# The first layer of the second MLP in float16 parts, its weights converted during the first MLP and kept in DRAM

## The chip, the cores and the metric

One core of one Trainium2 chip. The metric is the device time of one execution in microseconds, the median of the runs shown. Five engines work side by side, each with its own queue: PE (matrix products), DVE (vector), ACT (scalar functions), POOL, and SP, which issues all the DMAs of this kernel.

## The reference

```python
def _moe_ref(x, w_in, w_out):
    h = x @ w_in
    g = np.maximum(0.01 * h, h)
    return (g @ w_out).astype(np.float32)

def _moe2_ref(x, w_in, w_out):
    h = x @ w_in
    g = h * (1.0 / (1.0 + np.exp(-h)))
    return (g @ w_out).astype(np.float32)
...
    attn_out = _attn_ref(**attn_kwargs)
    x = np.ascontiguousarray(attn_out.transpose(0, 2, 1, 3)).reshape(B * S, H * D)
    x = _moe_ref(x=x, **moe_kwargs)
    return _moe2_ref(x=x, **moe2_kwargs)
```

The attention has 4 x 8 heads of 576 positions and 64 columns with a mask by blocks of 64. Both MLPs have 2304 tokens, a model width of 512 and an inner width of 2048. The weights come as 64-bit floats, everything else as 32-bit floats.

## The kernel before

The tokens are cut into six blocks of 384, numbered 0 to 5. The work has four stages on PE. First comes the attention of block 0 and the first MLP of block 0 in full precision. Then blocks one to five of the first MLP run while PE also works on the attention of the next block; each block has 16 steps (one per 128 inner columns), and a step is 12 products of the first layer (lines 1785 to 1787) and 12 of the second (line 1814). Each float32 operand there is a sum of two float16 parts, high and low, and a product is three matmuls: low by high, high by low, high by high.

Stage three is the first layer of the second MLP. It takes two blocks at a time (b = 0, 1, 2; 768 tokens) and two of the 16 inner tiles at a time (pair i = 0 to 7), and replaces the eight products of a 2 x 2 split by seven, after Strassen and Winograd, at the price of sums of operands and results. `add_first(b, i)` (line 2051) is one such unit: seven products, each of two halves of the contraction by three matmuls, 42 in all, of 128 x 384 (lines 2064 to 2066). Its operands are kept as high and low parts of type float32r. The sums over the results are made by DVE (lines 2089 to 2100), then ACT applies the Silu (line 2116) and takes squares of the result (line 2125), from whose largest a scale for stage four is found. Stage four is the second layer, again with seven products, in float16 parts (line 2243).

The order on each engine is written out ahead by a planner (`Schedule`, line 73). Every operation is a task with its possible engines and their estimated times, its dependencies and a rank; an engine that comes free takes the ready task of the lowest rank. Products of PE that belong to the two MLPs keep the order of the program (`in_turn`). A rank with `GATE` (-1000) is first, with `SHORT` (-500) next; then come plain ranks. A plain rank is the number of the step (block times 16 plus step) plus an offset, or, in stage three, `unit3(b, i)`, 96 plus 1.75 a unit. The attention's tasks have `rank_at`, made of `ATT` and `ATT_SLOPE`.

What the change touches, by name and line:

- `convert` (432) loads 128 x 512 weights of 64 bits (512 KB) into one of three `raw` places and makes 32-bit floats of them: a scaling on ACT (449), a shift on DVE or ACT (454, 456), and a join on DVE (460). It takes turns in two `cy` and two `cc` places.
- `first_pair(p)` (748) converts the two inner tiles of a pair for the first layer, makes four sums on DVE (`s1` to `s4`, 256 columns each) and splits 3.5 x 512 columns into high (402) and low (413) parts of float32r, all of it after the attention has ended. `last_raw(p)` (789) converts those of the second layer during stage three, takes their squares (806) and stores the four pieces in DRAM (`w2_kept`). `last_pair(p)` (924) reads them back and splits them by `scaled_split` (704: high part at 710, on ACT alone; low part at 715, on DVE) into places that earlier units have freed; its rank has `GATE`.
- `find_range` (851) turns a set of sums of squares into a power of two: a maximum over columns (DVE), a spread (ACT or DVE), a DMA transpose, another maximum and four one-column operations (DVE).
- `x_operands(b)` (1989) loads the first MLP's results for two blocks, makes four sums and splits seven operands of 768 columns into the `x3` places, which have one buffer each: for b > 0 an operand is rewritten after its last use in unit (b - 1, 7) and before its use in unit (b, 0).
- `add_second` (1876) is a step's second layer; in a block's last step it also evacuates four banks into y (1921, 1923) in places given by `YRINGS`, and stores them.

```python
                for k in (0, 1):
                    w, x = slice(k * P, (k + 1) * P), slice(k * n, (k + 1) * n)
                    nc.tensor.matmul(o, wlo[:, w], xhi[:, x], start=k == 0, stop=False)
                    nc.tensor.matmul(o, whi[:, w], xlo[:, x], start=False, stop=False)
                    nc.tensor.matmul(o, whi[:, w], xhi[:, x], start=False, stop=k == 1)
```

Of the kernel before, what the change touches and what calls it, by code (L numbers as in the profile page):

```python
# [19 lines left out]
P = 128  # L20
# [10 lines left out]
LATE = 10  # L31
# [18 lines left out]
W2_BEFORE, W2_MID = 2, 5  # L50
W2_AHEAD, X2_AHEAD, X2_FIRST, LAST_AHEAD = 18, 7, 14, 5
LAST_FROM, LAST_TO = 1, 14
# [193 lines left out]
def attn_mlp_mlp(  # L246
# [110 lines left out]

    def next_s():
        return ps_s.tile([P, 512], F32, tag="s", name="s")
# [69 lines left out]
    raws, cys, ccs = Turns(RAWS), Turns(CYS), Turns(CCS)  # L429

    def convert(src, f, sl, rk, load_rank, to=None, slow=0, lag=0, free=()):
# [4 lines left out]
        raw_free, raw_after, raw_users = raws.next()  # L436
# [3 lines left out]
        def load():  # L440
            r = raw_room().bitcast(I64)
# [23 lines left out]
        t_load = dma(raw_free, load_rank, DM * P * 8, load, after=[*raw_after, *raw_later], slow=slow, lag=lag)  # L465
        raws.takers.append(t_load.issue)
# [184 lines left out]
    class Place:  # L651


        def __init__(self, make, deps):
            self.make, self.deps, self.tile, self.halves = make, deps, None, None

        def view(self, a, n):
            if self.tile is None:
                self.tile = self.make(F32R)
            return self.tile[:, a : a + n]  # L660

        def half(self, a, n):
            if self.halves is None:
                self.halves = self.make(F16)
            return self.halves[:, 2 * a : 2 * a + n]

    def second_places():

        if w2_places:
            return  # L670
        for k in range(LATE - 1):
            place = Place(lambda t, k=k: late(k, t), [end_of_attention])
            w2_places.extend([(place, 0), (place, DM)])
        w2_places.append((Place(lambda t: late(LATE, t, n=DM), [end_of_attention]), 0))
        place = Place(lambda t: area("xw", "r" if t == F32R else "rh", t), ())
        place.step = slot_of("xw")[-1]
        w2_places.append((place, 2 * TWO))
        for k in (27, 28, 29, *range(9), *range(11, NF)):
            place = Place(lambda t, k=k: slot(k, "r" if t == F32R else "rh", t), ())
            place.step = k  # L680
            w2_places.extend([(place, 0), (place, DM)])
        assert len(w2_places) == 7 * NF // 2 - 2
        place = Place(lambda t: late(LATE - 1, t), ())
        place.step = None
        w2_places[7 * NF // 2 - 2 :] = [(place, 0), (place, DM)]

    def place_of(p, k, halved=False):

        second_places()
        at, over = 7 * p + k, 0  # L690
        if halved and (at == 2 * LATE - 1 or p % 2 == 0 and k == 6):
            at, over = at - 1 if k < 6 else at - 3, DM
        place, at = w2_places[at]
        deps = place.deps
        if hasattr(place, "step"):
            deps = y_there[NBLK - 2][:2] if place.step is None else slot_free(place.step)
        if halved:
            return deps, (lambda n=DM, a=0: place.half(at, over + a + n)[:, over + a :])
        return deps, (lambda n=DM, a=0: place.view(at + a, n))
# [3 lines left out]
    def high_on(n):  # L703
        return {"ACT": act(n, False, 1)}
# [18 lines left out]
    def seven_parts(p, whole, piece, rk, more=()):  # L723

        deps, get = zip(*(place_of(p, k) for k in range(7)))
        got, tasks = [], []
        for k, (n, value, t) in enumerate(whole):
            hi, lo = get[2 * k], get[2 * k + 1]  # L730
            ts = split(n, value, lambda hi=hi, lo=lo: (hi(), lo()), [*t, *deps[2 * k], *deps[2 * k + 1], *more], rk)
            got.append((hi, lo))
            tasks.append(ts)
        make, value = piece
        t4 = make(tasks)
        last = get[6]
        ts = split(H2, value, lambda: (last(H2), last(H2, H2)), [t4, *deps[6], *more], rk)
        tasks.append(ts)

        def operand(k, half):  # L740
            if k == 3:
                return last(H2), last(H2, H2)
            hi, lo = got[k]
            return hi(H2, half * H2), lo(H2, half * H2)

        return operand, tasks, t4

    w2_places = []
    w2_first, w2_last, w2_done1, w2_done2 = {}, {}, {}, {}

    def first_pair(p):

        rk = unit3(0, p) - W2_AHEAD
# [9 lines left out]
        def s2(e):  # L763
            rest(e, d["t"][:, H2:], d["t"][:, :H2], d0["x"][:, :H2])
# [1691 lines left out]
```

## Time and profile before

| | us |
|---|---|
| median of three runs | 877.36 (876.89 to 879.8) |
| the profiled execution | 878.52 |
| its span, first to last instruction | 876.8 |
| PE busy | 860.7 |
| DVE busy | 751.4 |
| ACT busy | 623.8 |
| matmuls | 6569 |

The page gives busy times over the whole span. The views by stretch, the chain of waits and the timelines show where the span goes. A matmul's own duration in the profile overlaps the next one's, so that the pace of PE is read from the distance of starts.

### The profile page before, as it was taken

Reading aid. Unit: us, or ns where it says so; the run is one execution under the profiler, and the core shown is the slowest. Engines: PE = TensorE matmul, PEld = TensorE weight load, DVE = VectorE, ACT = ScalarE, POOL = GpSimd, SP = SyncE. Lnnn points to the kernel's source line nnn. Section 1 sums busy time; section 2 is a strip of 40 time slices with the busy share of each in tenths; the row PEclk is TensorE's granted clock in tenths of the full one; section 3 lists DMA queues with packets and bytes.
Section 4 is the critical chain, followed back from the end, with each engine's and each line's share of the span. In section 5 each row is a group of like instructions: output and inputs, shape, how many; then the busy total and the mean of one; then the engine's idle time right before and its main releaser. Section 6 shows DMA issues by size and latency. Waiting matters only on the chain.

```text
span 876.8 us, 18274 instructions
## 1 busy us (share of the span) xinstructions
PE 860.7 (98%) x6569; PEld 648.6 (74%) x6569; DVE 751.4 (86%) x1700; ACT 623.8 (71%) x1434; POOL 14.9 (2%) x75
## 2 busy tenths in 40 slices
PE   8899999999999999999999999999999999999997
PEld 4655566666666666666666668999999978888886
DVE  6899989999988998888847399888787999998976
ACT  6899987777766877777636368898897985444433
POOL 0000000000000000000000000000000000000000
PEclk9999999999999999999999999999999999999999
DMA  8689866667776679764534145687858784544431
GB/s 292 212 210 280 238 149 167 135 137 144 174 175 130 141 156 196 165 150 119 109 107 145 71 137 189 231 283 266 290 194 270 271 254 136 177 144 133 159 108 61
DMA packets 179467, 155.77 MB, mean 178 GB/s; under 512 B 108592, under 2 KB 155440, under 8 KB 179376
## 3 DMA queue, kind: packets, MB, share of 16 engines
q1 hardware_dynamic: 179376, 154.61, 63.2%
q8 instruction: 51, 0.84, 0.4%
q14 instruction: 40, 0.33, 0.1%
HBM read 93.85 MB, written 35.65 MB: 148 GB/s over the span
## 4 chain that ended last, share of the span: by engine, by line
PE 79%; DVE 9%; ACT 6%; DMA 3%; issue 2%; DVEq 0%; POOL 0%; ACTq 0%; POOLq 0%; SPq 0%
PE acc L1814 11%; PE acc L2243 7%; PE h L1785 5%; PE h L1787 5%; PE h L1786 5%; PE s L2243 5%; PE s L1479 4%; PE u L1814 4%; PE h L1780 3%; PE x L1329 3%; DMA raw<-w 3%; PE u L2243 2%; PE acc L2065 2%; PE acc L2066 2%; PE acc L2064 2%; PE x L2243 2%
## 5 line engine op out<-in xcount | busy, mean ns | idle before, releaser
L1814 PEld LDWEIGHTS <-w 128*128 128x128 f16 x840 | 77.9, 98 | 52.2 <-issue 2.0
L1814 PE MATMUL acc<-ghi,w 128*128 128x384 f16 x420 | 103.1, 327 | 0.0
L1497 ACT ACTIVATE p<-s,st 128x288 f32<-128x288 f32 (+4 forms) x120 | 62.3, 521 | 45.1 <-DVE st L1489 36.1
L1785 PE MATMUL h<-h,w 128*128 128x384 f16 x280 | 91.9, 328 | 0.0
L1786 PE MATMUL h<-l,w 128*128 128x384 f16 x280 | 91.3, 326 | 0.0
L1787 PE MATMUL h<-h,w 128*128 128x384 f16 x280 | 91.3, 326 | 0.0
L1844 ACT ACTIVATE g<-h,wd 128x384 f32<-128x384 f32 x80 | 46.1, 577 | 46.9 <-PE h L1787 46.2
L1479 PE MATMUL s<-k,q 128*128 128x288 f32 (+5 forms) x288 | 77.4, 363 | 0.4 <-ACT p L1497 0.2
L1814 PE MATMUL acc<-glo,w 128*128 128x384 f16 x210 | 68.5, 326 | 0.0
L413 DVE TENSOR_TENSOR glo<-g,ghi 128x384 f16<-128x384 f32 x80 | 44.2, 553 | 26.5 <-ACT ghi L402 25.8
L1511 ACT ACTIVATE hl<-p,st 128x576 f16<-128x576 f32 (+5 forms) x89 | 53.9, 625 | 14.8 <-ACT p L1497 3.4
L1516 DVE SCALAR_TENSOR_TENSOR hl<-p,st,hl 128x576 f16<-128x576 f32 (+4 forms) x96 | 58.2, 624 | 5.3 <-ACT hl L1511 4.8
L2243 PEld LDWEIGHTS <-y 128*128 128x128 f16 x525 | 51.2, 98 | 9.4 <-issue 2.0
L1479 PEld LDWEIGHTS s<-k,q 128*128 128x128 f32 x288 | 47.0, 189 | 11.8 <-ACT p L1497 2.8
L2243 PEld LDWEIGHTS <-x 128*128 128x128 f16 x492 | 48.0, 98 | 6.7 <-DVE x L715 0.8
L2125 ACT ACTIVATE h<-e 128x384 f32<-128x384 f32 x96 | 46.8, 488 | 1.6
L2116 ACT ACTIVATE e<-e 128x384 f32<-128x384 f32 (+1 forms) x72 | 42.4, 622 | 7.5 <-DVE e L2096 6.0
L449 ACT ACTIVATE cy<-raw 128x512 f32<-128x512 f32 x64 | 42.2, 666 | 2.6 <-DMA raw<-w 2.0
L1785 PEld LDWEIGHTS <-w 128*128 128x128 f16 x280 | 27.3, 98 | 20.9 <-issue 4.4
L1787 PEld LDWEIGHTS <-w 128*128 128x128 f16 x280 | 27.4, 98 | 18.1
L402 ACT ACTIVATE ghi<-g 128x384 f16<-128x384 f32 x76 | 39.6, 521 | 1.2
L1786 PEld LDWEIGHTS <-w 128*128 128x128 f16 x280 | 27.5, 98 | 14.9
(355 smaller groups left out, 2329.9 us busy)
## 6 DMA issues: line engine op xcount, KB each, us to landing
raw<-w SPq DMA_DIRECT2D x64, 512.0 KB, 5.1
raw<-g SPq DMA_DIRECT2D x64, 256.0 KB, 3.2
g<-e SPq DMA_DIRECT2D x48, 192.0 KB, 3.6
g<-e SPq DMA_DIRECT2D x24, 384.0 KB, 3.3
kqr<-kq_l SPq DMA_DIRECT2D x16, 480.0 KB, 4.0
kqr<-kq_l SPq DMA_DIRECT2D x16, 416.0 KB, 3.4
y<-yT SPq DMA_DIRECT2D x12, 384.0 KB, 4.5
l<-w2k SPq DMA_DIRECT2D x18, 256.0 KB, 4.4
```

Of the source, the lines that this page charges most:

```text
L413: engine[e].tensor_tensor(lo, x, hi, op=ALU.subtract)
L1479: nc.tensor.matmul(s[:, :w], hd.q[:, a : a + P], hd.k[:, k0:k1], start=i + j == 0, stop=i == len(hds) - 1 and j == 1,)
L1497: nc.scalar.activation(p[:rows, k0:k1], u.s[piece][:rows, :w], AF.Exp, bias=nm[:rows], accum_out=s2[:rows, piece : piece + 1])
L1511: nc.scalar.activation(hl[:rows, 0, :n], p[:rows], AF.Copy, scale=rc[:rows])
L1516: nc.vector.scalar_tensor_tensor(hl[:rows, 1, :n], p[:rows], rc[:rows], hl[:rows, 0, :n], op0=ALU.mult, op1=ALU.subtract)
L1785: nc.tensor.matmul(h, w1_lo[s.f][:, sl], hi[:, c, : s.n], start=c == 0, stop=False)
L1786: nc.tensor.matmul(h, w1_hi[s.f][:, sl], lo[:, c, : s.n], start=False, stop=False)
L1787: nc.tensor.matmul(h, w1_hi[s.f][:, sl], hi[:, c, : s.n], start=False, stop=c == NC - 1)
L1814: nc.tensor.matmul(s.acc[c][:, : s.n], a, b, start=s.f == 0 and i == 0, stop=s.f == NF - 1 and i == 2)
L1844: nc.scalar.activation(s.g, s.h[:, :n], AF.Prelu, alpha=LEAK, scale=w_downs[:, at : at + 1])
L2125: nc.scalar.activation(h_all[:, :n], out_()[:, at : at + n], AF.Square, scale=SQUARE, accum_out=sum_at(col))
L2243: nc.tensor.matmul(o, a[:, x], b, start=i == 0 and j == 0 and q == 0, stop=i == NP - 1 and q == 2, skip_group_check=True,)
```

## The change

- The weights of stage three's first layer are converted, measured (squares and `find_range`) and summed in `w2_raw(0, p)`, which the program places behind steps 36, 41, 46, 51, 56, 61, 66 and 71 (block two, step 4, to block four, step 7) with a rank of the step plus 110. The four pieces of a pair are stored in DRAM. The loads have three places of their own (`e`).
- `first_pair` reads the pieces back (four loads a pair) and splits them into scaled float16 parts; `first_unit` says where they lie.
- `x_operands` takes squares of the four loaded y parts (eight a call), finds their range, and splits the seven operands into scaled float16 parts. The Silu takes the factor that undoes both scales from a column (`scalar_at(38 + b)`).
- The second layer's conversion, `w2_raw(1, p)`, is placed before units 3 to 10, and `last_pair(p)` after units 14 to 21, without `GATE`, into places that block five's steps have freed (`last_unit`). It reads two stretches of 1024 and 768 columns through the `raw` places.
- `scaled_split` may put the high part on DVE too. The evacuations of y in blocks one to four go to places of slots 27 and 28, in block five behind the x tiles. `ATT` goes from 44 to 64 and `ATT_SLOPE` from 0.8 to 0.95.

```diff
-ATT0, ATT1, ATT, ATT_SLOPE, AHEAD, V_LATE = 11.0, 0.3, 44.0, 0.8, 7.5, 0.0
+ATT0, ATT1, ATT, ATT_SLOPE, AHEAD, V_LATE = 11.0, 0.3, 64.0, 0.95, 7.5, 0.0
...
-YRINGS = ("rrry", "cycy", "cycy", "cycy", "llcy", "wwww")
+YRINGS = ("rrry", "ssss", "ssss", "ssss", "ssss", "wwww")
...
-LAST_FROM, LAST_TO = 1, 14
+FIRST_AT = (36, 41, 46, 51, 56, 61, 66, 71)
+RAW_AT = (3, 4, 5, 6, 7, 8, 9, 10)
+PAIR_AT = (14, 15, 16, 17, 18, 19, 20, 21)
+FIRST_RANK = 110.0
...
     def high_on(n):
-        return {"ACT": act(n, False, 1)}
+        return {"ACT": act(n, False, 1), "DVE": dve2x(n, 1)}
...
+    def w2_raw(which, p, rk, own=False, follow=()):
...
         both = [
             convert(
-                w2, 2 * p + i, slice(DM, 2 * DM), rk, rk - CONV_LOAD / 4, room[i], lag=LAG, free=busy
+                w2, 2 * p + i, cols, rk, rk - CONV_LOAD / 4, room[i], lag=LAG, free=load_users[at],
+                own=own, follow=follow,
             ) for i in (0, 1)
         ]
...
+            def squared(e, di=di, i=i):
+                nc.scalar.activation(
+                    di["r"][:, i * DM : (i + 1) * DM], di["x"], AF.Square, scale=SQUARE,
+                    accum_out=sum_at((112, 96)[which] + 2 * p + i),
+                )
...
+            def store(k=k, n=n, di=di, name=name):
+                nc.sync.dma_start(out=w2_kept[which][p][:, k * DM : k * DM + n], in_=di[name][:, :n])
...
+    def first_pair(p):
+
+        rk = unit3(0, p) - W2_AHEAD
+        t_range, _, by, _ = ranges[4]
...
+            free = e_users[r] or [t for u in e_raws.users[-3:] for t in u]
+            t_in = dma([w2_there[0, p][k], *free], rk - LAST_AHEAD, P * n * 4, load, lag=LAG)
...
+        operand, done = split_pieces(pieces, units_of(first_unit, p), by, t_range, rk)
...
+        for k, n in ((0, 2 * DM), (2, DM + H2)):
+            free, after, users = raws.next()
...
+        find_range(5 + b, (128 + 8 * b, 8), y_sq, rk - 20)
...
-            done[m] = split(TWO, value, lambda: x3_parts(m), [*deps, *free], rp)
+            done[m] = scaled_split(TWO, value, lambda: x3_parts(m), by, [*deps, *free, t_by], rp)
...
-            t[m] = in_turn(6 * mm(n), deps, rk, product)
+            t[m] = in_turn(6 * mm16(n), deps, rk, product)
...
-                nc.scalar.activation(out_(), out_(), AF.Silu)
+                nc.scalar.activation(out_(), out_(), AF.Silu, scale=scalar_at(38 + b))
...
+            if blk * NF + f in FIRST_AT:
+                w2_raw(0, FIRST_AT.index(blk * NF + f), step_of(blk, f) + FIRST_RANK, True, [s.before.t_g1])
+                if blk * NF + f == FIRST_AT[-1]:
+                    find_range(4, (112, 16), squares[3], step_of(blk, f) + FIRST_RANK)
```

## Rows read from the trace of the kernel before

**Rows 1.** The page, busy time by engine (share of the span) and instructions.

```profile
PE 860.7 (98%) x6569; PEld 648.6 (74%) x6569; DVE 751.4 (86%) x1700; ACT 623.8 (71%) x1434; POOL 14.9 (2%) x75
```

**Rows 2.** Busy time by stage: stretch, length, engines' busy us, PEclk, DMA share, GB/s.

```profile
215.00:455.00 240.00, 239.89 (x2216) 158.28 (x2214) 201.93 (x574) 169.06 (x420) 8.52 (x41) 1.00 0.66 145
455.00:521.00 66.00, 66.00 (x409) 39.72 (x407) 44.15 (x89) 35.73 (x68) 0.00 (x0) 1.00 0.35 117
521.00:704.00 183.00, 179.57 (x1029) 176.33 (x1028) 158.94 (x270) 156.34 (x381) 0.00 (x0) 1.00 0.75 251
704.00:760.00 56.00, 53.61 (x487) 47.41 (x487) 55.61 (x88) 35.22 (x55) 0.00 (x0) 1.00 0.60 188
```

**Rows 3.** Chain of waits in block five: start us, us, what.

```profile
480.52 1.46 PE acc L1814 x9
...
515.62 1.46 PE acc L1814 x9
```

**Rows 4.** Chain of waits in stage three.

```profile
532.94 0.17 PE x L2064
...
554.78 0.17 PE x L2064
```

**Rows 5.** Timeline of PE: start us, us, what [idle before <-releaser].

```profile
529.53 0.44 PE L2064 MATMUL acc<-l,w 128*128 128x384 f32 x1 [1.46 <-ACT l L1921]
...
647.73 0.44 PE L2065 MATMUL acc<-l,w 128*128 128x384 f32 x1 [0.41 <-DVE l L413]
...
704.52 1.47 PE L2243 MATMUL s<-w,y 128*128 128x256 f16 x12 [1.36 <-DVE e L2089]
...
715.59 0.61 PE L2243 MATMUL s<-w,x 128*128 128x256 f16 x4 [0.53 <-DVE x L715]
...
746.40 0.61 PE L2243 MATMUL s<-w,y 128*128 128x256 f16 x4 [1.16 <-DVE y L715]
```

**Rows 6.** Groups by form: names, shapes, count | busy us, mean ns | idle before.

```profile
L449 ACT ACTIVATE cy<-raw 128x512 f32<-128x512 f32 x64 | 42.2, 666 | 2.6 <-DMA raw<-w 2.0 <-DVE w L413 0.5
...
L456 DVE TENSOR_SCALAR cc<-raw 128x512 uint32<-128x512 uint32 x52 | 21.2, 421 | 4.5 <-DMA raw<-w 4.1
...
L460 DVE SCALAR_TENSOR_TENSOR l<-cy,cc 128x512 uint32<-128x512 uint32 x20 | 13.6, 684 | 3.7 <-ACT cy L449 3.7
...
L761 DVE TENSOR_TENSOR t<-cc 128x256 f32<-128x256 f32 x8 | 3.4, 420 | 0.1
...
L806 ACT ACTIVATE h<-l 128x512 f32<-128x512 f32 x16 | 9.6, 598 | 2.6 <-DVE l L460 2.4
...
L806 ACT ACTIVATION_READ_ACCUMULATOR h<-l 128x1 f32 x16 | 3.0, 187 | 0.0
...
L413 DVE TENSOR_TENSOR w<-cc,w 128x512 fp32r<-128x512 f32 x16 | 11.0, 685 | 1.4 <-ACT w L402 1.4
...
L715 DVE SCALAR_TENSOR_TENSOR w<-l,t,w 128x512 f16<-128x512 f32 x18 | 12.9, 743 | 1.3 <-ACT w L710 1.3
...
L402 ACT ACTIVATE w<-t 128x512 fp32r<-128x512 f32 x6 | 3.8, 626 | 0.8 <-DVE t L413 0.8
...
L710 ACT ACTIVATE w<-t,t 128x512 f16<-128x512 f32 x2 | 1.4, 710 | 0.0
```

**Rows 7.** Timeline of PE at the end of the attention.

```profile
450.45 1.69 PE L1329 MATMUL x<-raw,vp 128*64 128x128 f16 x72
...
458.91 0.33 PE L1785 MATMUL h<-h,w 128*128 128x384 f16 x1
```

**Rows 8.** Groups of ACT by form: both table loads, squares in block 0.

```profile
L1631 ACT ACT_TABLE_LOAD x1 | 1.3, 1283 | 0.8 <-PEq L2446 0.8
...
L2116 ACT ACT_TABLE_LOAD x1 | 1.3, 1283 | 0.0
...
L518 ACT ACTIVATE wj<-x 128x512 bf16<-128x512 f32 x6 | 3.8, 632 | 0.9 <-DVE x L460 0.8
```

**Rows 9.** Groups of DVE from 704 to 760 us.

```profile
L715 DVE SCALAR_TENSOR_TENSOR w<-l,t,w 128x512 f16<-128x512 f32 (+1 forms) x12 | 7.6, 676 | 0.2 <-ACT w L710 0.2
```

More of the change, by code (lines that the diff above doesn't have):

```diff
@@ L463, in joined @@
             )
-        t_load = dma(raw_free, load_rank, DM * P * 8, load, after=[*raw_after, *raw_later], slow=slow, lag=lag)
-        raws.takers.append(t_load.issue)
+        first = emptied("e") if own and len(turns.users) <= turns.n else []
+        t_load = dma([*raw_free, *first], load_rank, DM * P * 8, load, after=[*raw_after, *(follow if own else raw_later)], slow=slow, lag=lag)
+        turns.takers.append(t_load.issue)
         t_y = plan.add({"ACT": act(DM) + 50}, [t_load, *cy_free], rk, scaled, cy_after)
@@ L649, in split_weights @@
             done.append([t_hi, t_lo])
[L651 to L699, printed above, removed]
+    late_units = {}
@@ L721, in scaled_split @@
         return [hi, lo]
[L723 to L746, printed above, removed]
@@ new lines, in w2_raw, with new_t @@
+            t_sq.append(plan.add({"ACT": act(DM) + 150}, [ti, *slot_free(29)], rk, squared))
+            di["raw"].append(t_sq[-1])
+        squares[3 + which] += t_sq
+        def new_t():
+            d["t"] = cy.tile([P, DM], F32, tag="cy", name="t")
+        def t1(e):
+            new_t()
+            if which:
+                rest(e, d["t"][:, :H2], d0["x"][:, :H2], d0["x"][:, H2:])
+            else:
+                engine[e].tensor_tensor(d["t"][:, :H2], d1["x"][:, :H2], d1["x"][:, H2:], op=ALU.add)
@@ L837, in last_raw @@
-        for k, n, value, t in pieces:
-            def store(k=k, n=n, value=value):
-                nc.sync.dma_start(out=w2_kept[p][:, k * DM : k * DM + n], in_=value())
-            there.append(dma([t], SHORT + rk, P * n * 4, store, lag=LAG))
-        load_users[p % 2] = [*there[:3:2], t_1, t_2, t_3, t_4, *t_sq]
-        t_users += [there[1], t_4]
-        d1["raw"].append(there[3])
-    squares, ranges = [[], [], [], []], {}
+        if which:
+            pieces = ((d1, "x", DM, in1), (d, "t", DM, t_2), (d0, "x", DM, t_3), (d1, "r", H2, t_4))
+        else:
+            pieces = ((d0, "x", DM, in0), (d1, "x", DM, t_3), (d, "t", DM, t_2), (d1, "r", H2, t_4))
@@ new lines, in w2_raw, with split_pieces, parts, operand @@
+        for k, (di, name, n, t) in enumerate(pieces):
+            def store(k=k, n=n, di=di, name=name):
+                nc.sync.dma_start(out=w2_kept[which][p][:, k * DM : k * DM + n], in_=di[name][:, :n])
+            there.append(dma([t], SHORT + rk, P * n * 4, store, lag=LAG))
+        load_users[at] = [*there[:3], t_1, t_2, t_3, t_4, *t_sq]
+        t_users += [there[1 if which else 2], t_2, t_4]
+        d1["raw"] += [t_4, there[3]]
+    def split_pieces(pieces, units, by, t_range, rk):
+        got, done = [], []
+        for (n, value, deps), (unit_deps, get) in zip(pieces, units):
+            def parts(n=n, get=get):
+                return (get[0](), get[1]()) if n == DM else (get[0]()[:, :H2], get[0]()[:, H2:])
+            done.append(scaled_split(n, value, parts, by, [*deps, t_range, *unit_deps], rk))
+            got.append(parts)
+        def operand(k, half):
+            cols = slice(half * H2, (half + 1) * H2)
+            return tuple(x[:, cols] for x in got[k]()) if k < 3 else got[k]()
+        return operand, done
@@ L2045, in x_operands @@
         y_users[:] = [[t_1, *ts1], [t_1, *ts7], [*ts4], [t_2, t_3, *ts3], [t_2, *ts5], [t_4, *ts6]]
+        for k in range(4):
+            y_users[k].append(y_sq[k])
     e3_free = [[], []]
```

325 lines of the change are left out of this document (162 added, 163 removed).

## Prediction

> **What bounds the kernel now.** I read the page first: TensorE (PE) is busy for 98% of the span, with the clock granted in full in every stage ([rows 1, 2], PEclk 1.00). Since a busy PE need not be a PE at its peak, the second view is the busy time by stage [rows 2]. Blocks two to five with the attention (215 to 455 us), block five alone (455 to 521), the first layer of the second MLP (521 to 704, "stage three") and its second layer (from 704, "stage four") have different neighbours: DVE is busy for 201.9 of 240 us, 44.2 of 66, 158.9 of 183 and 55.6 of the next 56; ACT for 169.1, 35.7, 156.3 and 35.2. Third, the chain of waits gives the pace of the matmuls. In block five nine steps of 24 float16 matmuls of 384 columns lie between 480.52 and 515.62, 35.10 us or 162.5 ns each [rows 3]. In stage three three units of 42 float32r matmuls of the same shape lie between 532.94 and 554.78, 21.84 us or 173.3 ns each [rows 4]. Fourth, PE's own waits in the timeline [rows 5]: 1.46 us where block five's results are evacuated, 0.41 us where the x operands change, and 1.36, 0.53 and 1.16 us where stage four begins. So until 521 PE is nearly seamless, stage three is paced by the matmuls themselves, and some 3 us are lost from 703 to 747 behind a DVE that has no idle time.
>
> **The change, part by part.**
>
> *The matmuls.* Stage three has 3 x 8 x 7 x 6 = 1008 of them. As float16 of the shape of [rows 3] each takes 162.5 instead of 173.3 ns: 1008 x 10.8 = 10.9 us, all of it on PE, which bounds the stage. This is the largest and surest term: the same operation runs in this trace with the same tile and type.
>
> The Trainium skill, "TensorE: Matmul & The Clock Gate", section "Back-to-back issue gap", speaks for more: it gives about 131 ns for a sustained stream of weight load and matmul at 512 columns. At that pace, taken as a ceiling for 384 columns, the term would be an estimated 1008 x 42 = 43 us. The trace disagrees: 384 columns, a quarter fewer, take 162.5 ns here.
>
> *What is moved.* Per pair of weight rows (eight pairs) the conversion is two ACT scalings of 666 ns, two DVE shifts of 421, two DVE joins of 684 and four DVE sums of 420 [rows 6]: DVE 3.9, ACT 1.3 us. Eight pairs make 31 us on DVE, 11 on ACT. They lie before between 455 and some 540 us; they now come behind steps 36 to 71, in the stretch up to 455. There DVE has 240 - 201.9 = 38 us idle and ACT 71. New with them are 16 squares of 598 + 187 ns on ACT, 12.6 us, and 32 stores on SP's queue; later 32 loads, in block five, where DMA is a third busy [rows 2]. On PE all this is nothing as long as the attention keeps ahead of the first MLP. That cover is visible: the last attention product of block five begins at 450.45 and lasts 1.69 us, block five's first product begins at 458.91 [rows 7], 6.8 us later; cutting the result into two float16 parts, by two operations of the length of a conversion's (some 0.65 us, [rows 6]), leaves 5.5. The moved operations have the lowest rank, so they fill gaps, but one that has begun holds its engine for up to 0.68 us. The transposes of the attention share their queue with sixteen moved loads of 512 KB and the new stores. No row shows this mix. From below the cost is nothing, since the gaps suffice; from above it is 9 us (the 72 units of blocks three to five, 24 a block, each 0.2 us later make 14.4, less the cover of 5.5). I take 1.5, nearer to nothing, because PE is busy for 239.89 of these 240 us beside a DVE that is already 84% busy [rows 2].
>
> The squares now stand among the attention's exponentials. In block 0 squares stand among exponentials too, and the run has two table loads, one at its start and one at the first Silu [rows 8]. So I charge nothing for the mixture; a load for each of sixteen squares and one back, at the row's 1283 ns, would be 41 us of ACT. The Trainium skill, "ScalarE: Activation LUTs", section "Table sets: the hidden batching unit", says that each change to a function of another set costs such a load; by that rule, the trace shows that these two functions share a set.
>
> *The weights in block five.* What is left of a pair there is four splits: the high part is dearer by a pointer (710 against 626 ns, [rows 6]) but may go to DVE now. For eight pairs ACT has at most 8 x 3.5 x 0.71 = 20 us and DVE about as much, beside 35.7 and 44.2 us of which the conversions go. It fits into 66 us; PE sees nothing.
>
> *The x operands.* For each pair of blocks there are eight new squares and a search for the largest value, well ahead of their use. But the seven operands have a single buffer: each is rewritten between its last use in unit 7 and its first in unit 0 of the next pair of blocks, and DVE must make seven low parts in about that time. Now each unit is 42 x 10.8 = 0.45 us shorter and each low part 0.06 us longer (743 against 685 ns at 512 columns, [rows 6]): 0.45 + 7 x 0.06 = 0.9 us tighter at each of the two changes. The wait there (0.41 us, [rows 5]) says that there is no slack to spend, so 2 us are lost; bounds 0 and 5 (each operand waiting for its whole high part, 7 x 0.71, once).
>
> *Into stage four.* Before, the second layer's weights can be split only when units of the last pair of blocks have freed their places, which leaves twelve of their low parts to DVE after 704 [rows 9]. With float16 halves they have places of their own and come eight to one units earlier. The waits of 1.36, 0.53 and 1.16 us [rows 5] are behind that backlog. I take 2.5 of the 3.05 as gone, bounds 0 and 3.
>
> *Stage three's start.* The 1.46 us remain: the evacuations still stand behind the first Silu with its table load of 1.28 us [rows 8].
>
> **Sum.** -10.9 - 2.5 + 2.0 + 1.5 = -9.9 us. The profiled execution takes 878.52 us, 1.72 more than its span of 876.8; so 868.6 on its account. It is 1.16 us above the median of 877.36, so against the median I forecast 867.5.
>
> **The rivals.**
>
> *The attention falls behind (the other side).* If each of those 72 units of the attention is later by half a moved DVE operation, 0.34 us, that is 24.5 us; less the cover of 5.5 it is 19 us of PE standing still, and the total is 877.4 - 11.4 + 19 = 885. It decides at (5.5 + 11.4) / 72 = 0.23 us per unit. For it: DVE would be at 233 of 240 us in that stretch. Against: these units overlap one another, and what does not fit can still be done in block five.
>
> *ACT becomes stage three's bound.* Its 156.3 us of before gain 16 squares (at most 12.6 us), 72 Silus dearer by 0.084 (6.0), 14 high parts (1.2) and the twelve high parts to the low ones of [rows 9] (about 8), and lose the conversion of two or three pairs (2.5 x 3.5 us by [rows 6], about 9): 175 us in a stage of 170. For it: this sum. Against: high parts may go to DVE, and ACT has 30 idle us in block five in which the second weights' conversion may begin. If it decides, stage three stays at its old length less a little, and only the 2.5 us of the transition are won: 875 to 880, about no change.
>
> *Half is given back.* Cost of the attention near its upper bound, or of the x operands near theirs: 870 to 874.5.
>
> *More is won.* No stall at the changes and none in the attention, 10.9 + 3 and a part of the 1.46 us at the start: 860 to 864.
>
> That the float16 rate fails, so that the change doesn't do what it says, gets no chance of its own, nor do matmuls faster than that or table loads among the squares: [rows 3, 8] stand against all three.
>
> **How the numbers follow.** Forecast (864.5 to 870): 0.48. Half given back (870 to 874.5): 0.16. More won: 0.13. No change by ACT: 0.12. Attention behind: 0.11. Likeliest is the first, 867.5. The range takes in the first two, three quarters of the third and half of the fourth, 861.5 to 877.5, and leaves out 0.2. A measurement of this kernel can tell about 0.3% from no change, 874.7 to 880.0: faster 0.77, same 0.12, slower 0.11.
>
> **What would show it.** Right: in stage three's timeline 42 matmuls in 6.83 us; no wait of PE over 0.5 us between 690 and 750; waits at the two changes of x operands of about 1 us each; block five begins within 2 us of 458.9. Wrong: a gap of PE ahead of block three, four or five, with score or value products of the attention behind it (the first rival), or, in stage three, waits of PE for ACT's copies of the first product with ACT busy for over 97% (the second). The forecast is also wrong if float16 operands meet a limit that the first MLP does not show.

## The result, and the profile after

The changed kernel takes 870.11 us (868.99 to 870.35), against 877.56 us for the kernel before measured beside it: a ratio of 0.9908, 95% interval 0.9888 to 0.9928. It is 0.9% faster. The forecast was 867.5, 2.6 us lower.

All readings of the changed kernel come from an execution of 870.35 us with a span of 868.58. First the page, busy time by engine (beside [rows 1]).

```profile
PE 850.0 (98%) x6569; PEld 572.2 (66%) x6569; DVE 767.1 (88%) x1750; ACT 633.6 (73%) x1494; POOL 14.8 (2%) x77
```

PE lost 10.7 us of busy time, near the 10.9 expected, and the span lost 8.2. DVE and ACT gained 15.7 and 9.8 us. Next the busy time by stage: stretch, length, then busy us of PE, PEld, DVE, ACT and POOL (with counts), PEclk, DMA share, GB/s. It answers to [rows 2]; the stage borders have moved with the work.

```profile
215.00:466.00 251.00, 245.85 (x2229) 158.93 (x2227) 228.14 (x645) 197.45 (x498) 8.34 (x41) 1.00 0.89 208
466.00:528.00 62.00, 62.00 (x384) 37.35 (x382) 50.32 (x96) 47.46 (x97) 0.00 (x0) 1.00 0.85 288
528.00:698.00 170.00, 166.51 (x1022) 99.78 (x1021) 142.00 (x242) 152.00 (x372) 0.00 (x0) 1.00 0.63 210
698.00:760.00 62.00, 62.00 (x569) 55.48 (x568) 56.66 (x84) 22.18 (x29) 0.00 (x0) 1.00 0.44 139
```

PE is no longer seamless up to block five: it is short of 5.2 us in the first row, where [rows 2] shows 0.1. It is seamless in the fourth, where [rows 2] shows 2.4 missing. The first products of each part, read from PE's timeline, give the account:

| | before, us | after, us | stretch before | stretch after | difference |
|---|---|---|---|---|---|
| block one starts | 132.93 | 132.14 | 132.93 | 132.14 | -0.8 |
| block five starts | 458.91 | 465.85 | 325.98 | 333.71 | **+7.7** |
| stage three starts | 521.17 | 528.25 | 62.26 | 62.40 | +0.1 |
| stage four starts | 702.33 | 698.25 | 181.16 | 170.00 | **-11.2** |
| end of the span | 876.80 | 868.58 | 174.47 | 170.33 | **-4.1** |

Before (first row) and after (second to fourth), PE's waits between block one and block five: what waited, what ended it, us in total, times, longest.

```profile
PE s L1479 <- ACT p L1497: 0.2, 1, 0.2
```

```profile
PE s L1449 <- ACT p L1467: 3.9, 7, 1.3
PE s L1449 <- DVE k L422: 1.1, 3, 0.6
PE x L1299 <- DMA raw<-hl: 0.4, 1, 0.4
```

That is eleven waits and 5.4 us instead of one of 0.2. In seven of them scores of the attention (s) wait for the exponentials (p) that free their banks, in three for a low part made on DVE (k), and once a value product waits for its transpose. The longest is 1.3 us. The first three, 0.9 us in all, lie at 204.84, 215.70 and 221.22 us, before any weight is converted; the kernel before with the new rank (`before_att`, below) has them too. In the distances between starts, 7.3 of the 7.7 us stand behind products of lines 1757 and 1784, with which a step's layers end, and 6.1 of these where a score comes next.

Stage three's gain is the pace. These two rows of the changed kernel's PE timeline are the first product of two units that follow one another, 42 matmuls apart:

```profile
553.09 0.33 PE L2054 MATMUL x<-x,w 128*128 128x384 f16 x1
...
559.92 0.33 PE L2054 MATMUL x<-x,w 128*128 128x384 f16 x1
```

6.83 us, or 162.6 ns each, against 173.3 in [rows 4]. The weight loads (PEld) show the change of type too: a load of float32r weights took 188 ns on average and the loads 176.33 of 183 us [rows 2]; a load of float16 takes 98 ns and the loads 99.78 of 170 us. That the loads set the old pace fits this, but no run shows it. PE's waits in that stage, same columns as above:

```profile
PE acc L2054 <- ACT l L1893: 1.7, 1, 1.7
PE acc L2055 <- DVE h L703: 1.4, 2, 0.8
PE acc L2054 <- DVE h L1895: 0.4, 1, 0.4
```

The first and third are the stage's start, the second the two changes of x operands. From 698 to 760 us PE's timeline has no idle time at all; the three waits of [rows 5] behind 704 are gone.

### The profile page after: what moved, and what is told of

It reads as the page before. It is cut to its first block, busy times and chain, and to the rows that moved or that the text cites. A ratio compares the mean times of both kernels' runs of the same rounds, so it can differ in the third digit from the quotient of the medians.

```text
span 868.6 us, 18465 instructions
## 1 busy us (share of the span) xinstructions
PE 850.0 (98%) x6569; PEld 572.2 (66%) x6569; DVE 767.1 (88%) x1750; ACT 633.6 (73%) x1494; POOL 14.8 (2%) x77
## 4 chain that ended last, share of the span: by engine, by line
PE 52%; DVE 12%; ACT 4%; issue 2%; DMA 0%; DVEq 0%; ACTq 0%
PE acc L2232 8%; PE acc L1784 6%; PE s L2232 5%; PE x L2232 3%; PE u L2232 3%; PE h L1755 3%; PE h L1757 2%; PE h L1756 2%; PE acc L2055 2%; PE acc L2056 2%; PE acc L2054 2%; PE u L1784 2%; DVE hl L1486 2%; PE s L2054 1%; PE s L1449 1%
## 5 line engine op out<-in xcount | busy, mean ns | idle before, releaser
L1784 PEld LDWEIGHTS <-w 128*128 128x128 f16 x840 | 78.7, 98 | 53.0 <-issue 2.4
L2232 PEld LDWEIGHTS <-y 128*128 128x128 f16 x741 | 72.6, 98 | 8.4
L698 ACT ACTIVATE y<-raw,w 128x768 f16<-128x768 f32 (+1 forms) x27 | 23.6, 874 | 51.1 <-PE acc L2232 40.9
L2106 ACT ACTIVATE e<-e,w 128x384 f32<-128x384 f32 (+1 forms) x72 | 48.8, 711 | 5.6 <-DVE e L2086 4.9
L2232 PEld LDWEIGHTS <-xw 128*128 128x128 f16 x483 | 47.2, 98 | 5.8 <-issue 0.3
L2055 PEld LDWEIGHTS <-w 128*128 128x128 f16 x318 | 31.1, 98 | 23.1 <-issue 2.7
L2056 PEld LDWEIGHTS <-w 128*128 128x128 f16 x318 | 31.1, 98 | 22.3 <-issue 1.8
L2054 PEld LDWEIGHTS <-w 128*128 128x128 f16 x306 | 29.9, 98 | 19.8
L1755 PEld LDWEIGHTS <-w 128*128 128x128 f16 x280 | 27.3, 98 | 20.8 <-issue 4.1
```

The lines of the kernel that those rows point to most:

```text
L1755: nc.tensor.matmul(h, w1_lo[s.f][:, sl], hi[:, c, : s.n], start=c == 0, stop=False)
L1784: nc.tensor.matmul(s.acc[c][:, : s.n], a, b, start=s.f == 0 and i == 0, stop=s.f == NF - 1 and i == 2)
L2106: nc.scalar.activation(out_(), out_(), AF.Silu, scale=scalar_at(38 + b))
L2232: nc.tensor.matmul(o, a[:, x], b, start=i == 0 and j == 0 and q == 0, stop=i == NP - 1 and q == 2, skip_group_check=True,)
```

## The experiments

Two questions were open. Why did blocks one to five lose 7.7 us where 1.5 were forecast? Three theories: A, the transfers (the DMA share from 300 to 386 us is 1.00 now); B, the moved work of DVE and ACT; C, the attention's new rank. And what removed the waits into stage four? Each run names its edit against the changed kernel, unless said otherwise, and each total is of one execution, except for `mid_evac` (five). "Stretch" is the time from block one's first product to block five's.

A yardstick first. Two kernels below (`late_pairs`, `pairs_held`) keep the changed kernel's order on DVE and ACT past 578 us, and one (`act_only`) up to 457. Their stretches are 332.2, 332.2 and 332.7, so the same order varies by about 1.5 us, and its mean, with the 333.7 above, is 332.7. The kernel before and `before_att` have 326.0 and 326.1. The change thus costs the stretch about 6.7 us, and the 7.7 of the execution shown above is the upper end.

**Thinning the moved work: `thin_engines`, `thin_dma`, `thin_both`.** For six of the eight pairs the moved conversions, squares and sums are cut to 8 columns, or the stores of six pairs and 13 of the 16 moved loads to 64 columns, or both. Where the stores are cut, the reading back takes what the first two pairs stored. All three keep the changed kernel's order of operations on PE, DVE and ACT.

```diff
-            nc.scalar.activation(d["y"], d["top"], AF.Prelu, alpha=2.0**32, scale=2.0**-112)
+            m = 8 if own and f > 3 else DM
+            nc.scalar.activation(d["y"][:, :m], d["top"][:, :m], AF.Prelu, alpha=2.0**32, scale=2.0**-112)
...
-            nc.sync.dma_start(out=r, in_=src[f, :, sl])
+            if own and f > 2:
+                nc.sync.dma_start(out=r[:, :64], in_=src[f, :, sl][:, :64])
+            else:
+                nc.sync.dma_start(out=r, in_=src[f, :, sl])
```

> The changed kernel, with the moved conversions, squares and sums of six of the eight pairs cut to 8 columns (so the weights of stage three are not the reference's); all DMAs keep their size, and every instruction its place. Theory A (DMA traffic): the stretch from block one to block five stays within 1 us of 333.7. Theory B (DVE and ACT work): it falls to 327 to 329, the whole to some 864 us. Theory C (rank): 333 to 334.

> The changed kernel, with 13 of the 16 moved weight loads and the stores of six of the eight pairs cut to 64 of their 512 columns (the weights of stage three are therefore not the reference's); every instruction, its place and its engine stay. The stretch from block one's first product to block five's first took 325.98 us before and 333.71 us after the change. Theory A (the moved DMA traffic delays the attention's transposes): the stretch falls to 327 to 329 and the whole to some 864 us. Theory B (the moved DVE and ACT work delays the attention): it stays at 332 to 334, the whole at 869 to 870. Theory C (the new rank of the attention does it): no change either, 333 to 334.

> Both cuts together (the weights of stage three are again not the reference's). Theories A and B, or both acting together: the stretch from block one to block five falls to 326 to 328, as before the change. Theory C (the written order and the attention's rank cost the time by themselves): it stays at 331 or more.

| | total, us | stretch, us |
|---|---|---|
| changed order, mean of four | | 332.7 |
| thin_dma | 872.20 | 332.15 |
| thin_engines | 866.85 | 329.53 |
| thin_both | 865.47 | 328.41 |

The windows from 300 to 386 us of the kernel before, the changed kernel, `thin_dma`, `thin_engines` and `thin_both`, one row each:

```profile
300.00:386.00 86.00, 86.00 (x766) 56.33 (x765) 75.34 (x216) 64.78 (x155) 4.94 (x23) 1.00 0.77 167
```

```profile
300.00:386.00 86.00, 83.57 (x740) 53.45 (x739) 80.01 (x229) 68.39 (x169) 4.41 (x22) 1.00 1.00 231
```

```profile
300.00:386.00 86.00, 83.69 (x742) 53.58 (x740) 80.19 (x231) 68.40 (x170) 4.47 (x22) 1.00 0.80 176
```

```profile
300.00:386.00 86.00, 85.20 (x753) 55.21 (x754) 75.83 (x241) 62.86 (x176) 4.39 (x22) 1.00 1.02 237
```

```profile
300.00:386.00 86.00, 85.86 (x760) 55.56 (x758) 76.63 (x240) 63.65 (x179) 4.78 (x23) 1.00 0.83 178
```

With the DMA share down from 1.00 to 0.80, near the 0.77 of the kernel before, PE is as short as in the changed kernel (83.69 and 83.57 of 86), and the stretch falls by no more than the same order varies. With DVE relieved of 4.2 us and ACT of 5.5, and the DMA share left at 1.02, PE gains 1.6 us in this window and the stretch 3.2. So theory A falls, as far as these runs can tell: thinning the transfers gives 0.6 us alone and 1.1 beside the other, both within what the same order varies. Theory B holds for a part: 3.2 of the 6.7 us, about half, go with the work of DVE and ACT of three quarters of the pairs, and 4.3 with both cuts. Neither stretch fell as far as forecast (327 to 329 us for DVE and ACT, 326 to 328 for both). What is left belongs to the last quarter and, perhaps, to the order itself, which these runs don't separate.

`thin_dma` is slower in all than its stretch says: block one begins 1.4 us later, and 1.7 us are lost at stage three's start. The rows are of PE's timeline:

```profile
536.52 0.43 PE L2058 MATMUL acc<-l,w 128*128 128x384 f16 x1 [1.71 <-ACT l L1897]
536.74 0.53 PE L2059 MATMUL acc<-l,w 128*128 128x384 f16 x1
537.06 0.53 PE L2060 MATMUL acc<-l,w 128*128 128x384 f16 x1
...
539.94 0.37 PE L2060 MATMUL acc<-h,w 128*128 128x384 f16 x1
540.15 0.33 PE L2058 MATMUL u<-l,w 128*128 128x384 f16 x1
```

Ten matmuls stand 0.32 us apart, half their pace: the granted clock from 536 to 540 is 0.58. In the changed kernel the same wait of 1.71 us, at the same place, is followed by full pace, 1.00. The fall costs some 1.6 us, and the wait alone doesn't decide whether it comes.

**The rank: `att_back`, `before_att`.** The old rank in the changed kernel, and the new one in the kernel before.

```diff
-ATT0, ATT1, ATT, ATT_SLOPE, AHEAD, V_LATE = 11.0, 0.3, 64.0, 0.95, 7.5, 0.0
+ATT0, ATT1, ATT, ATT_SLOPE, AHEAD, V_LATE = 11.0, 0.3, 44.0, 0.8, 7.5, 0.0
```

> The changed kernel with the attention's rank as before the change (44 and 0.8 in place of 64 and 0.95). Theory C (this rank delays the attention): the stretch from block one to block five falls from 333.7 to below 330 us. Theories A and B (load on DMA, or on DVE and ACT): it stays within 2 us of 333.7, and the whole within 868 to 872 us.

> The kernel before with the attention's new rank alone (64 and 0.95 for 44 and 0.8). In the changed kernel the old rank costs 9.7 us. If the new rank is better by itself, the stretch from block one's first product to block five's falls from 326.0 by up to 4 us, to 322 to 324, and the total is 873 to 876; then the moved work costs some 10 us and the rank hides a part of them. If it only serves the kernel with the moved conversions, the stretch is 325 to 328 and the total 876.5 to 880.

`att_back` takes 879.84 us, with a stretch of 337.75. Up to block four's first product it is, with 250.6 us, ahead of the changed kernel (254.8) and of the three kernels of its order (253.2, 253.3 and 254.4); then one wait loses it all. PE's timeline, then DVE's:

```profile
469.32 0.53 PE L1299 MATMUL x<-raw,vp 128*64 128x64 f16 x12 [6.74 <-DMA raw<-hl]
```

```profile
455.24 0.31 DVE L1483 TENSOR_SCALAR hl<-p,st 128x192 f16<-128x192 f32 x1
...
456.78 1.02 DVE L703 SCALAR_TENSOR_TENSOR x<-y,w,x 128x768 f16<-128x768 f32 x1 [0.70 <-ACT x L698]
...
464.17 1.02 DVE L703 SCALAR_TENSOR_TENSOR l<-y,w,l 128x768 f16<-128x768 f32 x1
465.10 0.41 DVE L1486 SCALAR_TENSOR_TENSOR hl<-p,st,hl 128x192 f16<-128x192 f32 x1
```

The last low part of the attention's probabilities stands on DVE behind eleven operations, most of them the splits of stage three's x operands. Its transpose, and with it the last value products, come 10 us late. That is the prediction's first rival, as one wait in place of 72 small ones. `before_att` takes 877.43 us beside 878.09 for the kernel before, with a stretch of 326.06: the rank alone changes nothing that could be measured. In the changed kernel it puts the splits of the x operands behind the attention's last parts, which matters once the moved work has brought the two close together. Theory C as stated, that the new rank by itself causes the loss, falls. Beside the moved work the rank does count: up to block four the old one is 2.6 to 4.2 us shorter (one run), so that a part of the loss there lies in the order that the new rank makes.

**The way into stage four: `late_pairs`, `pairs_held`.** The first emits the second weights' splits later; the second also makes them wait.

```diff
-PAIR_AT = (14, 15, 16, 17, 18, 19, 20, 21)
+PAIR_AT = (22, 22, 22, 22, 23, 23, 23, 23)
```

> The second layer's weights are split behind units 22 (four pairs) and 23 (four pairs) instead of one pair behind each of units 14 to 21; the work is the same. Theory (the waits into stage four of the kernel before were the backlog of these splits on DVE, and the gain of 4.1 us there comes from splitting earlier): the waits return, PE stands for 3 us or more between 695 and 750, and the total is 873 to 876. Rival (they came from the new matmuls' end or from the sums of the operands of stage four): PE loses under 1 us there and the total stays within 1 us of 870.

It takes 873.83 us, in the theory's range, but not for its reason: PE has no wait at all between 695 and 750, and the longer parts are block five (63.8 us) and stage three (172.0). Nothing of it speaks on the question, since the low parts of these weights begin between 582.0 and 670.1 us instead of 580.5 and 663.0. A place further down in the program doesn't delay a task that the planner finds ready. So:

```diff
-    def last_pair(p, rk):
+    def last_pair(p, rk, held):
...
+        pieces = [(n, v, [*ts, held]) for n, v, ts in pieces]
...
-                        last_pair(p, unit3(b, i))
+                        last_pair(p, GATE + unit4(0, i) - 4, t_unit)
...
-PAIR_AT = (14, 15, 16, 17, 18, 19, 20, 21)
+PAIR_AT = (16, 17, 18, 19, 20, 21, 22, 23)
```

> The run with the pairs behind units 22 and 23 did not put the second layer's splits late: they ended at 670 us, as in the changed kernel (663). Here the splits of pair p wait for the last product of unit 16 + p, and have the rank of the kernel before (GATE); the work and the places are those of the changed kernel. Theory (the waits into stage four came from splits that could start only when a unit of the last pair of blocks had ended): low parts of weights stand after 698 again, DVE has no idle time between 700 and 750, and PE loses 3 us or more there: 872 to 876. Rival (the waits came from something else, the order of the sums or the places of the operands of stage four): PE loses under 1 us between 695 and 750, and the total stays within 2 us of 870.

It takes 882.57 us, more than the theory gave. Rows of PE's and of DVE's timeline:

```profile
702.47 0.61 PE L2234 MATMUL x<-w,y 128*128 128x256 f16 x2 [6.20 <-ACT y L698]
703.52 1.03 PE L2234 MATMUL x<-w,y 128*128 128x256 f16 x4 [0.44 <-DVE y L703]
710.67 0.39 PE L2234 MATMUL s<-w,cc 128*128 128x256 f16 x2 [1.04 <-ACT cc L698]
712.42 1.03 PE L2234 MATMUL s<-w,cc 128*128 128x256 f16 x4 [1.36 <-DVE cc L703]
```

```profile
699.37 1.29 DVE L703 SCALAR_TENSOR_TENSOR w<-raw,w,w 128x256 f16<-128x256 f32 x2
...
702.45 1.02 DVE L703 SCALAR_TENSOR_TENSOR y<-raw,w,y 128x768 f16<-128x768 f32 x1
```

PE waits 9.0 us in four pieces, and the granted clock from 700 to 720 falls to 0.69. The operands of stage four come after the last weights on DVE, whose last low parts begin at 699.37 us. The expected sign that DVE has no idle time from 700 to 750 failed (it is busy for 44.7 of 50 us): the waits are at the start of stage four, and the clock adds to them. So splits that start late and then stand first in rank are enough to make PE wait here, and the changed kernel, which splits early, has no wait. That the kernel before's later waits, at 715 and 746 us, came from its twelve low parts after 704 [rows 9] fits this but is not shown by itself. A gain on the other side shows too: here both waits at the changes of x operands are gone, because the splits no longer fill DVE there, and stage three's last matmul starts at 695.94 after a first at 527.78, 168.2 us instead of 169.8.

**The second rival: `act_only`.** The high part on ACT only, as before.

```diff
     def high_on(n):
-        return {"ACT": act(n, False, 1), "DVE": dve2x(n, 1)}
+        return {"ACT": act(n, False, 1)}
```

> The high part of a weight may be made on ACT alone, as in the kernel before; the changed kernel makes 17 of them on DVE, 16 of them in stage three between 578 and 662. By the sum of the prediction's second rival ACT then has about 152 + 16 x 0.7 = 163 us of 170 in stage three. If ACT's work bounds the stage once its share comes near the whole, stage three lengthens by 2 us or more and waits of PE for ACT's copies of the first product appear: 872 to 876. If only the share is high and nobody waits, stage three keeps its 170 us and the total stays within 1 us of 870.

It takes 873.33 us. From 528.82 to 701.07 stage three has 172.25 us instead of 170.00. ACT is busy for 159.1 of the 172 us from 528 to 700 (152.4 in the changed kernel). PE's waits there:

```profile
PE acc L2054 <- ACT l L1893: 1.7, 1, 1.7
PE s L2055 <- DVE x L703: 1.4, 1, 1.4
PE acc L2055 <- DVE h L703: 1.0, 1, 1.0
PE acc L2054 <- DVE e L2086: 0.8, 1, 0.8
PE acc L2054 <- DVE h L1895: 0.6, 1, 0.6
```

The stage lengthens by about the 2 us that the rival asked for, but not by waits for ACT's copies of the first product: low parts of x come later, and a sum of results once. `late_pairs`, whose ACT is not burdened, has 172.0 us there as well, with the same wait for x (1.5 us). That points to the order at the change of x operands rather than to ACT's share; one run of each doesn't settle it.

**Moving the conversions: `spread`, `spread_mid`.**

```diff
-FIRST_AT = (36, 41, 46, 51, 56, 61, 66, 71)
+FIRST_AT = (36, 43, 50, 57, 64, 71, 78, 82)
```

> The conversions of the first layer's weights stand further apart: behind steps 36, 43, 50, 57, 64, 71, 78 and 82 instead of 36 to 71 by fives; nothing else is changed, and the work is the same. Theory B (the 7.7 us that blocks one to five lose are the moved work of DVE and ACT): two of eight pairs now come where block five's matmuls need little else of DVE and ACT, and the others leave wider gaps, so the stretch from block one's first product to block five's shortens from 333.7 to about 332, block five and stage three keep their lengths, 868 to 869 in all. Rival (the work only changes place): what comes after 455 delays the splitting of the first weights, stage three begins with a wait of 2 us or more on a split, and the total is 870 or above.

The stretch shortens as expected, to 331.4, and yet the total is 881.67 us. PE waits for 9.8 us in one piece, and then runs at half pace. A row of PE's timeline, two of ACT's, and windows:

```profile
548.01 0.48 PE L2054 MATMUL s<-x,w 128*128 128x384 f16 x1 [9.83 <-DVE e L2079]
```

```profile
544.85 0.72 ACT L698 ACTIVATE x<-e,w 128x512 f16<-128x512 f32 x1 [3.12 <-DMA e<-w2k]
545.48 0.49 ACT L698 ACTIVATE xw<-e,w 128x256 f16<-128x256 f32 x1
```

```profile
538.00:548.00 10.00, 0.17 (x2) 0.00 (x0) 5.70 (x16) 4.45 (x9) 0.00 (x0) 0.68 0.88 268
548.00:552.00 4.00, 3.99 (x13) 1.92 (x13) 3.08 (x5) 3.96 (x8) 0.00 (x0) 0.51 0.33 124
```

The releaser named, a sum on DVE, follows the weights: ACT had waited for the reading back (e<-w2k) until 544.85. The range of the first weights needs the squares of the last pair, so a late last conversion makes all splits late: the first split of these weights begins at 494.75 us instead of 462.18. Hence a middle course:

```diff
-FIRST_AT = (36, 41, 46, 51, 56, 61, 66, 71)
+FIRST_AT = (36, 42, 48, 54, 60, 66, 70, 74)
```

> The eight conversions behind steps 36, 42, 48, 54, 60, 66, 70 and 74 instead of 36 to 71 by fives; the work is the same. The wide spread (to step 82) shortened the stretch from block one to block five by 2.3 us and lost 12.5 us in stage three, where the second unit's weights came from DRAM 10 us late. If that loss needs the last conversion to end after the attention, the last one here (step 74, about 425 us) is early enough: stretch 332 to 333, stage three 170, 868.5 to 870 in all. If the reading back is late already, PE waits for e in the first units of stage three and the total is above 871.

The stretch is 329.6 us, 3.1 under the mean of the changed order: the same work at other steps gives back about as much as thinning it did. The total is 870.67: block five grows to 64.1 us, with waits for ACT and DVE at 477 to 479, and stage three to 172.2, with 11 matmuls at half pace behind the wait of its start (granted clock 0.79 from 536 to 540).

**POOL for the sums: `pool_sums`.**

```diff
+        sums = {"DVE": dve(H2)} if which else {"POOL": 900}
-        t_1 = plan.add(on_vector(H2), [in0 if which else in1, *t_free], rk, t1, t_after)
+        t_1 = plan.add(sums, [in0 if which else in1, *t_free], rk, t1, t_after)
```

The other three sums change in the same way.

> The four sums of each moved pair (32 operations of 256 columns, about 13 us of DVE) go to POOL, which is busy for under 20 us of the whole span; nothing else is changed. Theory B (DVE's and ACT's time is what the 7.7 us are): DVE falls by some 5 us in 300 to 386, the stretch shortens by 13 of the 43 us moved to the two engines times 4.2 to 5.6 us (what thinning three quarters of them or all would give), about 1.5 us: 332, 868.5 in all. Rival (POOL's sums are slow, or slow DVE down beside them): the conversions end late or DVE's operations lengthen, and the stretch is 334 or more: 870 and above.

It takes 879.78 us, with a stretch of 335.9. DVE has 76.2 us from 300 to 386 instead of 80.0, and from block one to block four it takes 250.9 us, 3.9 less than the changed kernel and 3.0 less than the mean of its order. The planner also orders the operations otherwise from 251 us on, so that this gain is not DVE's time alone. Then the long wait of `att_back` comes again: a wait of 4.0 us for a transpose (raw<-hl) before block five, with the attention's last parts behind the splits of x on DVE. A sum of 256 columns takes 754 to 920 ns on POOL, 420 on DVE [rows 6]. The Trainium skill, "GPSIMD Engine Reference", section "3. Performance versus the Vector engine", gives about twice DVE's time for such an addition, of 2048 columns; this trace agrees (1.8 to 2.2 times).

**Both findings together: `mid_evac`.** The steps of `spread_mid`, and block five's evacuations on DVE only, which is idle for 3.58 us while ACT has the squares, the table load and the Silu ahead of them.

```diff
+            if blk == NBLK - 1:
+                time = {"DVE": dve_psum(n) + 61}
```

> Two edits: the conversions behind steps 36 to 74, as in the run before with those steps, and the four evacuations of block five's results on DVE alone. In the changed kernel three of the four stand on ACT behind the squares of the x operands, the table load of 1.28 us and the first Silu, while DVE is idle for 3.58 us and PE waits 0.39 and 1.71 us; in the run with steps to 74 that wait is followed by 11 matmuls at 0.32 us instead of 0.16. Theory: these waits are ACT's queue and nothing else, so on DVE the evacuations follow one another within 0.6 us, PE loses under 0.5 us there, no matmul is at half pace, and with the stretch of that run (329.6 us instead of 333.7) the total is 865 to 867.5. Rival for the place: PE waits as long for something else behind (the banks' sums on DVE, weights from DRAM), 868 to 870. Rival for the stretch: the 4.1 us of that run do not come again, 868 to 870 too, but with blocks one to five at 333 us or more.

It takes 869.28 us (868.83 to 871.49), a ratio of 0.9908 to the kernel before, interval 0.9892 to 0.9924: the same as the changed kernel, and not the theory's 865 to 867.5. The stretch is 331.0 us. The waits of stage three's start fall from 2.1 to 1.4 us, without half pace, where the theory gave under 0.5: PE now waits for the evacuations on DVE. Block five gives it back: it lasts 66.5 us. ACT's timeline, then PE's:

```profile
477.06 0.72 ACT L698 ACTIVATE w<-e,w 128x512 f16<-128x512 f32 x1 [2.74 <-DMA e<-w2k]
477.68 0.51 ACT L411 ACTIVATE ghi<-g 128x384 f16<-128x384 f32 x1
```

```profile
478.24 0.48 PE L1784 MATMUL acc<-ghi,w 128*128 128x384 f16 x2 [1.60 <-ACT ghi L411]
479.08 0.48 PE L1784 MATMUL acc<-glo,w 128*128 128x384 f16 x1 [0.36 <-DVE glo L422]
479.35 0.85 PE L1784 MATMUL acc<-ghi,w 128*128 128x384 f16 x2
479.99 0.53 PE L1784 MATMUL acc<-glo,w 128*128 128x384 f16 x1
```

The split of a weight stands ahead of block five's own cut on ACT and waits 2.74 us for its reading back. PE waits for the cut and then runs at half pace for some 3 us, with a granted clock of 0.57 from 479 to 483. `spread_mid`, with the same order up to here, has 1.35 us of that wait of ACT, 1.1 us of PE's and no half pace. The rows above are of an execution of 871.38 us with a mean granted clock of 0.997; three of the other four have 1.000 and take 868.83 to 869.28 us, so the fall is not in each of them. No version here that does all of the work is shown to beat the changed kernel.

## Why the prediction was nearly right

The direction and the largest term were right; three smaller terms were off, and partly against one another.

- *The matmuls*, -10.9: right. A unit takes 6.83 us, as the prediction said.
- *What is moved*, +1.5: this is the term that was mis-sized. It measures +7.7 (about 6.7 over the runs of the same order), near the upper bound of 9. The step that failed is the choice of 1.5 "because PE is busy for 239.89 of these 240 us beside a DVE that is already 84% busy": that a cover has held says nothing of how much of it is left. DVE went from 88% to 93% from 300 to 386 us, and scores waited for exponentials there. Block five begins at 465.85, so that the sign "within 2 us of 458.9" failed. It is the first rival's mechanism in small pieces, on average 0.11 us over 72 units. The cover of 5.5 us that the prediction took off did not help: the visible distance between the start of the attention's last product and block five, 8.5 us in [rows 7], is still there (9.4 now, 456.42 to 465.85), but PE lost the time in single waits along the way, before that cover came into play. Thinning shows that DVE's and ACT's work makes about half of the 6.7 us, and that the transfers count little. The rest stays open: other steps for the same work (`spread_mid`) shorten the stretch by 3 us too, and the old rank beside it (`att_back`) shortens the part up to block four by 2.6 to 4.2.
- *The attention falls behind*: not in the changed kernel, but in two neighbours (`att_back`, `pool_sums`). It decides by the order of one operation at the attention's end, not by a sum of small delays as the rival had it.
- *The weights in block five*, 0: right for the changed kernel (62.40 against 62.26 us). In `mid_evac`, whose last conversions come later, the same splits cost PE 2.0 us of waits. The cover is the time from reading back to use.
- *The x operands*, +2.0: too dear. The prediction read one wait of before (0.41 us). Read by starts, the units at the two changes took 7.68 and 8.43 us before, where a unit takes 7.28, and take 7.57 and 7.78 now, where one takes 6.83: 1.55 us were lost and 1.70 are, so +0.15. The waits alone make 1.4 us instead of 0.6. The shorter unit and the longer low parts, which the prediction priced, cost nothing by themselves: the splits of the second weights fill DVE there, as `pairs_held` shows, which has both and no wait at the changes.
- *Into stage four*, -2.5: the place was right, the size is -4.1. All three waits of [rows 5] went, and one of 0.18 us at 708.14. Read by starts, these four cost 3.9 us (1.63, 0.46, 0.80 and 1.43 us from one matmul to the next, in place of 0.11); the other 0.2 lie behind the last matmul's start. That late splits can make such waits is shown by `pairs_held`.
- *Stage three's start*, 0: right. The waits there are 1.7 and 0.4 us against 1.46 and 0.18, but the first unit, with the products of block five in it, takes 11.19 us against 11.61, which is the new pace and no more.
- *ACT as stage three's bound*: ACT has 152 of 170 us, not the 175 of the rival's sum. Both arguments against it held. The choice of DVE for the high parts is worth some 7 us, as `act_only` shows, where ACT has 159 of 172. The larger part is the second weights' conversion that block five takes: in stage three ACT makes 5 scalings and 6 squares of weights, where it made 21 and 16 before.

The sum of the measured differences is -0.8 + 7.7 + 0.1 - 11.2 - 4.1 = -8.2 us (rounded terms make -8.3), where -9.9 was forecast. The moved work cost 6.2 us more. Stage three gave 2.3 us more (-11.2 against -10.9 + 2.0): 1.85 are the x operands, and 0.45 a unit near 690 us in which PE waited for a sum of results before and no longer does. The way into stage four gave 1.6 more. The last 0.8, block one's earlier start, belongs to no term: kernels of the same order begin block one between 132.1 and 133.8 us. That the total came within 2.6 us of the forecast is in part luck: the moved work alone was off by 6.2, and other terms by 3.9 the other way. (The sum compares the two profiled executions; by the medians the change is -7.4 us.)

## What to carry to other kernels

Work that is moved under a "busy" neighbour isn't free because the bounding engine has shown no waits so far; price it by what the feeding engines have left (here DVE went from 84 to 91% busy). Here the upper half of the bounds would have been right. Where the work is placed counts as well: other steps for the same work gave back some 3 us of the stretch, and then lost them behind it. When work is moved earlier, look for the one consumer at the border, the last piece of the earlier stage and the first read-back of the next, and whether the planner can put a waiting operation ahead of it. And an operation that is to come late needs a dependency: a later place in the program did not delay it.

## What was unexpected of the hardware

After some waits PE ran at half its pace for 6 to 16 matmuls of 384 columns (0.32 us instead of 0.16): the granted clock was 0.58 from 536 to 540 in `thin_dma`, 0.51 from 548 to 552 in `spread`, 0.50 from 470 to 475 in `att_back`. That is the lower of the two levels, 1.2 GHz of 2.4. It added 1 to 3 us to each such wait. Behind 130 us it followed all four waits of 4 us and more in these traces (4.01, 6.20, 6.74 and 9.83 us). It followed a wait of 1.71 us in one kernel and not the same wait in six others, and the same two waits, of 2.40 and 0.67 us, in `att_back` (granted clock 0.57 from 543 to 547) and not in `pool_sums`. So the price of a short wait is not its length alone, and no run here tells which short waits are followed by it.
